# A mixture-of-experts stage on two weight buffers: slots 2 and 3 go to the first buffer, slots 20 and 21 to the second

## The chip, the cores and the metric

The kernel runs on one core of a Trainium2 chip. The metric is the device time of one execution in microseconds. The times before are three runs: 948.5, 950.81 and 951.74 us, median 950.81. The profile is of one further execution that took 946.81 us, of which 945.0 us are the profiled span.

## The reference

Three layers, one after the other: attention, a dense feed-forward layer, and a mixture of experts (the one that the change touches).

```python
scores = scale * np.matmul(q, k.transpose(0, 1, 3, 2))           # 4 x 8 heads, 576 x 64
thresh = np.max(scores, axis=-1, keepdims=True) - tau            # keep what is near the maximum
scores = np.where(scores >= thresh, scores, -1000000000.0)
x = softmax(scores) @ v                                          # -> 2304 tokens x 512
h = x @ w_in;  x = (np.maximum(h, 0.0) + np.log1p(np.exp(-np.abs(h)))) @ w_out   # 512 -> 2048 -> 512
e_idx = np.argmax(x @ w_gate, axis=1)                            # one of 8 experts for each token
for e in range(E):
    mask = e_idx == e
    h = np.maximum(x[mask] @ w1[e], 0.0)                         # 512 x 1024
    ye = h @ w2[e]                                               # 1024 x 512
    out[mask] = gate_w[mask, None] * eom[mask, e, None] * ye
```

## The kernel before

Attention and the feed-forward layer take the first three quarters of the span and are the same in both kernels. The mixture of experts follows. Its tokens are sorted on the chip by expert into slots of up to 128 tokens, each slot with one expert. With these inputs 22 slots run (0 to 21, `MAIN`); three more stand behind a condition (L1374) and are skipped. Slots 0 and 1 (`NPRE`) belong to the expert with the most tokens, chosen before the last two token tiles are routed. The other slots are columns of a table that the kernel computes at about 700 us; column `c` of the table has an expert (`z.esi`), a flag that a new expert begins there (`z.chi`, also set at column `LANE` = 10), and the token numbers (`z.idx`).

One slot goes through these steps:

- `gather` (L1144): GpSimd fetches the slot's rows from DRAM by an indirect transfer into one of five buffers `xg`; `rows` (L1154) transposes them into `xgT` by a transfer on the sync engine's queue.
- `load_w` (L1163): eight transfers of 512 KB on the sync engine's queue, four for the first weight matrix and four for the second, into a ring of 12 raw buffers. They are conditional: where the flag is not set, the transfer is issued without moving anything. A load waits until the conversion that used its raw buffer 12 loads earlier is done.
- `conv_w` (L1178): the conversion of float32 weights into two float16 parts. ScalarE writes the high part (L1195), VectorE the low part (L1200). Both stand in a conditional on the slot's flag (`changed`, L1135), so that they run only where a new expert begins; passing an untaken one costs a branch and an event.
- `up` (L1210): 96 matmuls of 128 columns (L1224) give `hps`; they read all four chunks of the first matrix.
- `relu` (L1234): in two halves, ScalarE (L1238) and then VectorE (L1241) make `hT` in two parts.
- `down` (L1249): 24 matmuls of 512 columns (L1260) give `yps`; block j of eight needs chunk j // 2 of the second matrix.
- `out_y` (L1268): ScalarE scales `yps` into `y` (L1274), GpSimd scatters it to the output (L1277).

There are two buffers of expert weights, `WA` (0) and `WB` (1), each with both matrices. `buf_of` says which slot uses which, `col_of` which column it works on: slots with buffer 0 walk through columns 0 to 9, those with buffer 1 through columns 10 to 19, so that two runs of columns alternate. `before(u)` is the last slot ahead of u with the same buffer; slot u's weights may be written only when that slot's `up` (first matrix) or `down` (second) is done:

```python
u = before(s)
free = (ff1_s, ff2_s)[buf_of(s)][len(groups) - 1] if u is None else (up_s if m == 1 else down_s)[u]
```

A planner (class `Planner`) orders the instructions of each engine from costs and due times, but from slot 2 on (`on`, `FREE`) the order on each engine is that of the code: `chain` makes a step wait for the one called before it on its engine. The loop at L1346 therefore writes the order. In period s stand: the output of slot s-1, the first half of the conversions of slot s+2's first matrix, `up` and the first relu half of slot s+1, the second half of those conversions, the second relu half, the conversions of slot s+1's second matrix, `down` of slot s. TensorE's order is so up(s+1), down(s), up(s+2), down(s+1). `queue` holds the loads in the same order.

Of the kernel before, what the change touches and what calls it, by code (L numbers as in the profile page):

```python
# [49 lines left out]
class Planner:  # L50
# [26 lines left out]
    def at(self, t, fn):  # L77
        self.n += 1
        heapq.heappush(self.events, (t, self.n, fn))
# [77 lines left out]
def attention_ff_moe_kernel(ctx, tc, q, k, v, tau, w_in, w_out, wg, wog, w1, w2, out):  # L157
# [15 lines left out]
    KC = DM // P  # L173
    FC = FF // P
    F2C = F2 // P
    NPRE = 2
# [115 lines left out]
    def step(*a, **kw):  # L292
        return plan[0].step(*a, **kw)
# [673 lines left out]
    MAIN = NU - 3  # L967

    LANE = (MAIN - NPRE) // 2
# [23 lines left out]
    def vec(dur, due, fn, after=(), take=(), drop=()):  # L993
        return step("DVE", dur, due, fn, after, take, drop)
# [109 lines left out]
    flag = {}  # L1104
    queue = []

    def col_of(u):
        return u - NPRE if u >= MAIN else (u - NPRE) // 2 + (LANE if u % 2 else 0)

    def buf_of(u):  # L1110
        return 0 if u <= NPRE else 1 if u >= MAIN else u % 2

    def before(u):

        return next((v for v in range(u - 1, -1, -1) if buf_of(v) == buf_of(u)), None)

    def row_of(u):
        return z.idxp[:, u:u + 1] if u < NPRE else z.idx[:, col_of(u):col_of(u) + 1]

    def when(s):  # L1120
        return D0 + DS * s
# [7 lines left out]
    def chain(on, eng, dur, due, fn, after=(), take=(), drop=(), **kw):  # L1129
        s = step(eng, dur, due, fn, list(after) + ([tail.get(eng)] if on else []), take, drop, **kw)  # L1130
        if on:
            tail[eng] = s
        return s
# [10 lines left out]
    def gather(s, on, after):  # L1144
        xg_b[s] = S_xg.buf(2)

        def fn():
            n = NB * P if s < NPRE else NT
            nc.gpsimd.indirect_dma_start(out=z.xg[s % NG], out_offset=None, in_=x2d[0:n, :], in_offset=bass.IndirectOffsetOnAxis(ap=row_of(s), axis=0),
                                         bounds_check=n - 1, oob_is_err=False)  # L1150

        g_s[s] = chain(on, "POOL", 1.1, when(s) - GAD, fn, after, [xg_b[s]], dma=0.73)

    def rows(s, on):  # L1154
        def fn():
            xgT[s] = z.p2.tile([P, 2 * KC, P], F16, tag="xgT", name="xgT", bufs=XGB)
            nc.sync.dma_start_transpose(out=xgT[s], in_=z.xg[s % NG][:, 0:DM].bitcast(F16))

        b = S_xgT.buf(1)
        n = 2 * KC  # L1160
        tr_s[s] = chain(on, "SP", 0.39 + 0.112 * n, when(s) - XGD, fn, [g_s[s]], [b], [xg_b[s]], dma=0.112 * n), b
# [16 lines left out]
    def conv_w(i, n, on):  # L1178

        ks = range(i, i + n)  # L1180
        m, s, c0 = queue[i]

        def part(k):
            c = queue[k][2]
            w = weights(m, s)
            w = w[:, :, c] if m == 1 else w[:, :, c * JW:(c + 1) * JW]
            r = z.raw[k % RWB]
            return w, r if m == 1 else r.rearrange("p (j d) -> p j d", d=DM)

        sc = SE1 if m == 1 else SE2  # L1190

        def hi():
            for k in ks:
                w, r = part(k)
                nc.scalar.activation(w[:, 0], r, AF.Copy, scale=sc)  # L1195

        def lo():
            for k in ks:
                w, r = part(k)
                nc.vector.scalar_tensor_tensor(out=w[:, 1], in0=r, scalar=sc, in1=w[:, 0], op0=ALU.mult, op1=ALU.subtract)  # L1200

        u = before(s)
        free = (ff1_s, ff2_s)[buf_of(s)][len(groups) - 1] if u is None else (up_s if m == 1 else down_s)[u]
        sd = when(s) - (SPD if m == 1 else SPE) + 0.02 * c0
        a = chain(on, "ACT", n * CVA, sd, lambda: changed("ACT", s, hi), [load_s[k] for k in ks] + [free, flags.get((s, "ACT"))])
        v = chain(on, "DVE", n * CVD, sd, lambda: changed("DVE", s, lo), [a, flags.get((s, "DVE"))])
        for k in ks:
            conv_s[queue[k]] = a, v

    def up(s, on):  # L1210
        xt, t_b = tr_s[s]
        w = [conv_s[1, s, c][1] for c in range(KC) if (1, s, c) in conv_s]
        d = when(s)
        p = up_s.get(s - 1)

        def mm1(hf, i):
            if i == 0:
                hps[s, hf] = z.ps_h.tile([P, 4, P], F32, tag="h", name="hps")
            w1b = weights(1, s)
            for f4 in (2 * i, 2 * i + 1):  # L1220
                c = (4 * hf + f4) * P
                for n in range(3 * KC):
                    wl, xl = THREE[n % 3]
                    nc.tensor.matmul(hps[s, hf][:, f4, :], w1b[:, wl, n // 3, c:c + P], xgT[s][:, xl * KC + n // 3, :], start=n == 0, stop=n == 3 * KC - 1)  # L1224

        for hf in range(2):
            ps_of[s, hf] = S_h.buf(1)
            for i in range(2):
                p = chain(on, "PE", 1.34, d, lambda hf=hf, i=i: mm1(hf, i), [p, xt] + w, [ps_of[s, hf]] if i == 0 else [], [t_b] if hf and i else [])
            h_s[s, hf] = p  # L1230
        up_s[s] = p


    def relu(s, hf, on):  # L1234
        def hi():
            if hf == 0:
                hT[s] = z.p2.tile([P, 2, F2C, P], F16, tag="hT", name="hT")
            nc.scalar.activation(hT[s][:, 0, 4 * hf:4 * hf + 4], hps[s, hf], AF.Relu)  # L1238

        def lo():  # L1240
            nc.vector.scalar_tensor_tensor(out=hT[s][:, 1, 4 * hf:4 * hf + 4], in0=hps[s, hf], scalar=0.0, in1=hT[s][:, 0, 4 * hf:4 * hf + 4],  # L1241
                                           op0=ALU.max, op1=ALU.subtract)

        if hf == 0:
            hT_b[s] = S_hT.buf(1)
        a = chain(on, "ACT", 0.55, when(s), hi, [h_s[s, hf]], [hT_b[s]] if hf == 0 else [])
        hl_s[s, hf] = chain(on, "DVE", 0.6, when(s), lo, [a], drop=[ps_of[s, hf]])
# [20 lines left out]
    def out_y(s, on):  # L1268
        y_b = S_y.buf(1)
        x = {}  # L1270

        def fn():
            x["o"] = z.p2.tile([P, DM], F32, tag="y", name="y")
            nc.scalar.activation(x["o"], hps[s, 2], AF.Copy, scale=z.xg[s % NG][:, DM:DM + 1].bitcast(F32))  # L1274

        def scatter():
            nc.gpsimd.indirect_dma_start(out=out, out_offset=bass.IndirectOffsetOnAxis(ap=row_of(s), axis=0), in_=x["o"], in_offset=None,  # L1277
                                         bounds_check=NT - 1, oob_is_err=False)

        a = chain(on, "ACT", 0.57, when(s) + DND, fn, [down_s[s]], [y_b], [y_ps[s], xg_b[s]])  # L1280
        y_s[s] = chain(on, "POOL", 1.1, when(s) + DND, scatter, [a], drop=[y_b], dma=0.73)
# [7 lines left out]
    def slot_flag(s, name, eng):  # L1289
        c = col_of(s)  # L1290
        flag[name, s] = eng.value_load(z.chi[0:1, c:c + 1], min_val=0, max_val=1)
# [15 lines left out]
    s = step("PE", 0.39, -1, pre_rows, [ps] + oh_s[:NB], [f_b])  # L1307
    s = vec(0.47, -1, pre_index, [s], drop=[f_b])
# [4 lines left out]
    s = vec(1.2, -1, table_slots, [te])  # L1313
    s = vec(0.55, -1, table_ones, [s])
    f_b = S_f.buf(1)
    s = step("PE", 0.5, -1, table_rows, [s] + oh_s, [f_b])
    ti = vec(0.64, -1, table_index, [s], drop=[f_b])
    se = vec(2.45, -0.5, slot_experts, [ti])
    table = [ti, opened] + [x2_w[t] for t in range(NTT)]
# [9 lines left out]
    def fill():  # L1329

        while len(load_s) < min(len(conv_s) + RWB, len(queue)):
            i = len(load_s)
            expert_of(queue[i][1])
            load_w(i, True)

    def convs(m, s, c, on):
        if (m, s, c) in queue:
            conv_w(queue.index((m, s, c)), 2, on)
            fill()


    for s in range(1, MAIN):
        queue += [(1, s + 2, c) for c in range(KC) if s + 2 < MAIN] + [(2, s + 1, c) for c in range(KC) if NPRE < s + 1 < MAIN]
    for i in range(0, 2 * KC, 2):
        conv_w(i, 2, False)
    for s in range(NPRE - 4, MAIN):  # L1346
        on = s >= FREE
        if s > 0:
            out_y(s - 1, on)
        if s + 4 < MAIN:  # L1350
            gather(s + 4, True, table)
        if NPRE <= s + 3 < MAIN:
            rows(s + 3, True)
        if s >= 0:
            fill()
        if s >= 1:
            convs(1, s + 2, 0, on)
        if 0 <= s + 1 < MAIN:
            up(s + 1, on)
            relu(s + 1, 0, on)  # L1360
        if s >= 1:
            convs(1, s + 2, 2, on)
        if 0 <= s + 1 < MAIN:
            relu(s + 1, 1, on)
        if s >= 1:
            for c in range(0, KC, 2):
                convs(2, s + 1, c, on)
        if s >= 0:
            down(s, on)
    out_y(MAIN - 1, True)  # L1370
# [54 lines left out]
```

## Time and profile before

| what | value |
|---|---|
| median of three runs | 950.81 us (948.5 to 951.74) |
| profiled execution | 946.81 us, span 945.0 us |
| TensorE (PE) busy | 803.4 us, 85% of the span |
| VectorE (DVE) busy | 640.5 us, 68% |
| ScalarE (ACT) busy | 601.0 us, 64% |
| GpSimd (POOL) busy | 477.1 us, 50% |

Busy shares are means over stages with different limits, so the change is looked for in its own stage, from about 700 us on. In the page's second part each digit is the busy share of 1/40 of the span (23.6 us) in tenths; `PEclk` is the clock granted to TensorE in tenths of full speed. In a timeline the number in brackets is the idle time of the engine ahead of the row and what ended it.

### The profile page before, as it was taken

What the parts mean: (1) busy time and instruction counts of PE and PEld (TensorE: products, weight loads), DVE (VectorE), ACT (ScalarE), POOL (GpSimd) and SP (SyncE); (2) the same over time, 40 slices, a digit from 0 to 9 for tenths busy, and PEclk for the clock granted to TensorE, in tenths of its full rate; (3) what the DMA queues carried; (4) which work ended last, traced back from release to release, by engine and by line L of the source; (5) the groups of instructions that cost most, each with busy time, mean ns of one, the idle gap of its engine ahead of it and who ended that gap; (6) DMA issues with size and microseconds to landing.
All of it is one profiled execution on the core that took longest, in us unless ns stands there. A gap on an engine that the chain in (4) does not pass through costs nothing. (4 is left out here: it accounts for less than half of the span.)

```text
span 945.0 us, 24188 instructions
## 1 busy us (share of the span) xinstructions
PE 803.4 (85%) x9138; PEld 562.4 (60%) x9138; DVE 640.5 (68%) x1403; ACT 601.0 (64%) x1000; POOL 477.1 (50%) x522
## 2 busy tenths in 40 slices
PE   1244677899889998999999999999894999999996
PEld 0023545567666665666666666666564777777774
DVE  3999999868898788777668575643672335239632
ACT  3665678777787877887777778745522335248532
POOL 2698787667676665775656757532211111122101
PEclk9997779999999999999999999999996999999998
DMA  9989877899999789877876675711729378399970
GB/s 206 238 195 213 207 178 166 170 151 176 199 174 182 139 161 178 166 136 119 146 133 109 126 151 82 127 38 34 235 61 272 106 259 182 93 266 350 253 213 34
DMA packets 353391, 156.45 MB, mean 166 GB/s; under 512 B 314350, under 2 KB 330734, under 8 KB 353264
## 3 DMA queue, kind: packets, MB, share of 16 engines
q1 hardware_dynamic: 349744, 145.33, 72.3%
q0 software_dynamic: 3520, 9.48, 3.6%
q8 instruction: 73, 1.20, 0.5%
q14 instruction: 54, 0.44, 0.2%
HBM read 120.66 MB, written 10.52 MB: 139 GB/s over the span
## 5 line engine op out<-in xcount | busy, mean ns | idle before, releaser
L695 PE MATMUL ph<-xT,WA 128*128 128x128 f16 (+1 forms) x2304 | 212.9, 252 | 14.6 <-ACT r L718 14.1
L591 POOL TENSOR_TENSOR es<-e,es 128x576 f16<-128x576 f32 x144 | 191.7, 1337 | 66.1 <-ACT es L587 61.9
L695 PEld LDWEIGHTS <-WA 128*128 128x128 f16 x2304 | 186.4, 101 | 44.9 <-issue 18.2
L705 PE MATMUL x2ps<-WB,gt 128*128 128x512 f16 x840 | 201.3, 382 | 1.9 <-POOL gt L733 1.1
L558 PE MATMUL sc<-kT,qT 128*128 128x512 f16 (+1 forms) x312 | 90.3, 401 | 71.3 <-DVE e L580 46.6
L580 DVE SCALAR_TENSOR_TENSOR e<-sc,th,e 128x576 f32<-128x576 f32 x140 | 112.0, 813 | 35.0 <-ACT e L575 25.6
L565 DVE TENSOR_REDUCE mx<-sc 128x1 f32<-128x576 f32 x140 | 102.2, 750 | 40.6 <-PE sc L559 37.6
L705 PEld LDWEIGHTS <-gt 128*128 128x128 f16 x840 | 75.5, 98 | 84.2 <-issue 3.9
L733 POOL TENSOR_TENSOR gt<-r,gt 128x512 f16<-128x512 f32 x70 | 83.7, 1196 | 79.5 <-ACT gt L730 71.1
L587 ACT ACTIVATE es<-e 128x576 f16<-128x576 f32 x144 | 98.0, 681 | 31.4 <-DVE e L580 24.3
L575 ACT ACTIVATE e<-sc,nb 128x576 f32<-128x576 f32 x140 | 99.8, 735 | 25.2 <-DVE nb L568 19.2
L1277 POOL DMA_INDIRECT out_dram<-y,idx x20 | 21.6, 1079 | 181.5 <-ACTq L1141 100.5
L603 PE MATMUL pv<-V,eT 128*128 128x64 f16 (+1 forms) x2400 | 85.3, 198 | 21.8 <-DMA eT<-es 16.4
L603 PEld LDWEIGHTS <-eT 128*128 128x128 f16 (+1 forms) x2400 | 80.2, 103 | 35.1 <-DMA eT<-es 26.0
L1241 DVE SCALAR_TENSOR_TENSOR hT<-hps,hT 128x512 f16<-128x512 f32 x44 | 30.2, 689 | 98.4 <-ACTq L1141 66.7
L558 PEld LDWEIGHTS <-qT 128*128 128x128 f16 (+1 forms) x320 | 30.1, 103 | 111.5 <-DVE e L580 45.7
L571 POOL TENSOR_SCALAR th<-mx,tau_s 128x1 f32<-128x1 f32 x144 | 65.2, 457 | 47.1 <-DVE mx L565 38.0
L1260 PEld LDWEIGHTS <-hT 128*128 128x128 f16 x528 | 50.6, 98 | 56.9
L1224 PE MATMUL hps<-xgT,WA 128*128 128x128 f16 x1152 | 69.0, 223 | 10.0 <-DMA xgT<-xg 9.9
L1224 PEld LDWEIGHTS <-WA 128*128 128x128 f16 x1152 | 67.6, 100 | 13.4 <-DMA xgT<-xg 9.5
L727 DVE SCALAR_TENSOR_TENSOR r<-l,r 128x512 f32<-128x512 f32 x72 | 58.1, 807 | 20.7 <-ACT l L724 20.5
L1238 ACT ACTIVATE hT<-hps 128x512 f16<-128x512 f32 x44 | 26.2, 596 | 70.3 <-PE hps L1224 69.9
(171 smaller groups left out, 1318.1 us busy)
## 6 DMA issues: line engine op xcount, KB each, us to landing
raw<-in_moe_w_dram SPq DMA_DIRECT2D x160, 512.0 KB
raw<-in_moe_w_in_dram SPq DMA_DIRECT2D x16, 512.0 KB
raw<-in_moe_w_out_dram SPq DMA_DIRECT2D x16, 512.0 KB
x2d<-row SPq DMA_DIRECT2D x18, 258.0 KB
rawq<-in_q_dram SPq DMA_DIRECT2D x16, 256.0 KB
rawk<-in_k_dram SPq DMA_DIRECT2D x12, 256.0 KB
rawv<-in_v_dram SPq DMA_DIRECT2D x24, 128.0 KB
eT<-es SPq DMA_TRANSPOSE x72
```

The lines of the kernel that those rows point to most:

```text
L558: nc.tensor.matmul(sc[r:r + n, o], w, main[:, :, :, h // 2, o].rearrange("p m x s -> p (m x) s"), start=pa == 0, stop=pa == 1)
L565: nc.vector.tensor_reduce(out=x["mx"], in_=x["sc"], axis=AX.X, op=ALU.max)
L571: nc.gpsimd.tensor_scalar(out=x["th"], in0=x["mx"], scalar1=tau_s, scalar2=None, op0=ALU.subtract)
L575: nc.scalar.activation(x["e"], x["sc"], AF.Exp, bias=x["nb"], scale=SCORE)
L580: nc.vector.scalar_tensor_tensor(out=x["e"], in0=x["sc"], scalar=x["th"], in1=x["e"], op0=ALU.is_ge, op1=ALU.mult, accum_out=sums[t][:, h: ...
L587: nc.scalar.activation(w["e"][:, 0, o * S:(o + 1) * S], x["ev"], AF.Copy)
L591: nc.gpsimd.tensor_tensor(out=w["e"][:, 1, cols], in0=x["ev"], in1=w["e"][:, 0, cols], op=ALU.subtract)
L603: nc.tensor.matmul(pv[t][r:r + n, h, :], eT[u][:, el, j + 4 * o, r:r + n], V[b][:, h // 2, j + 5 * o, vl, :], start=i == 0, stop=i == len( ...
L695: nc.tensor.matmul(ph[:, ci * w * P:(ci + 1) * w * P], WA[:, wl, k // 3, fc * P:(fc + 1) * P], xT[u[0]][:, xl * KC + k // 3], start=k == 0 ...
L705: nc.tensor.matmul(acc_ps[u[a]], gt[:, gl, c:c + P], WB[:, wl, fc, :], start=fc == 0 and m == 0, stop=fc == FC - 1 and m == 2)
L733: nc.gpsimd.tensor_tensor(out=gt[:, 1], in0=r, in1=gt[:, 0], op=ALU.subtract)
L1224: nc.tensor.matmul(hps[s, hf][:, f4, :], w1b[:, wl, n // 3, c:c + P], xgT[s][:, xl * KC + n // 3, :], start=n == 0, stop=n == 3 * KC - 1)
```

## The change

It assigns buffers and columns anew. Slots up to 2 have buffer 0, as before. Before, slot 3 had buffer 1, slot 4 buffer 0, and so on to slot 21 with buffer 1. Now slot 3 has buffer 0 as well, slot 4 buffer 1, slot 5 buffer 0, in turn to slot 19 with buffer 0 and slot 20 with buffer 1, and slot 21 has buffer 1 too. Columns follow: buffer 0 serves columns 0 to 9 with slots 2, 3, 5, 7, ..., 19 (before: 2, 4, ..., 20), buffer 1 columns 10 to 19 with slots 4, 6, ..., 20, 21 (before: 3, 5, ..., 21). Where a slot follows directly on another of its buffer (3 and 21), `in_period` puts its conversions one period later, since its buffer is in use until then. Gathers and scatters at the start come in another order.

```diff
+    def buf_of(u):
+        return 0 if u <= NPRE else 1 if u >= MAIN - 1 else (u - NPRE + 1) % 2
+
     def col_of(u):
-        return u - NPRE if u >= MAIN else (u - NPRE) // 2 + (LANE if u % 2 else 0)
-
-    def buf_of(u):
-        return 0 if u <= NPRE else 1 if u >= MAIN else u % 2
+        if u >= MAIN:
+            return u - NPRE
+        return sum(buf_of(v) == buf_of(u) for v in range(NPRE, u)) + (LANE if buf_of(u) else 0)
...
-    for s in range(1, MAIN):
-        queue += [(1, s + 2, c) for c in range(KC) if s + 2 < MAIN] + [(2, s + 1, c) for c in range(KC) if NPRE < s + 1 < MAIN]
+    def in_period(m, s):
+
+        def at(u):
+            near = before(u) == u - 1
+            return u - 2 + near if m == 1 else u - 1 + near
+
+        return [u for u in range(NPRE + 1, MAIN) if at(u) == s]
+
+    for s in range(MAIN):
+        queue += [(m, u, c) for m in (1, 2) for u in in_period(m, s) for c in range(KC)]
...
-        if s + 4 < MAIN:
-            gather(s + 4, True, table)
+        for u in {-1: (2,), 0: (3,), 1: (4,), 2: (5, 6)}.get(s, (s + 4,) if s > 2 else ()):
+            if u < MAIN:
+                gather(u, True, table)
...
-        if s >= 1:
-            convs(1, s + 2, 0, on)
+        w1s = [(u, c) for u in in_period(1, s) for c in range(0, KC, 2)]
+        n = sum(u == s + 1 for u, c in w1s) or 1
+        for u, c in w1s[:n]:
+            convs(1, u, c, on)
         if 0 <= s + 1 < MAIN:
             up(s + 1, on)
             relu(s + 1, 0, on)
-        if s >= 1:
-            convs(1, s + 2, 2, on)
+        for u, c in w1s[n:max(n, 2)]:
+            convs(1, u, c, on)
         if 0 <= s + 1 < MAIN:
             relu(s + 1, 1, on)
-        if s >= 1:
+        for u, c in w1s[2:]:
+            convs(1, u, c, on)
+        for u in in_period(2, s):
             for c in range(0, KC, 2):
-                convs(2, s + 1, c, on)
+                convs(2, u, c, on)
```

On ScalarE at the start of the stage, before: behind both relu halves of slot 2 (`hT`) stand slot 3's conversions into `WB`, then those of slot 4 into `WA`, ahead of the first relu half of slot 3. Each pair of conversions is in a conditional.

```order
L1238 ACTIVATE hT<-hps 128x512 x2
L1141 COMPARE_AND_BRANCH
L1195 ACTIVATE WB<-raw_10220 128x1024
L1195 ACTIVATE WB<-raw_10221 128x1024
L1141 UNCONDITIONAL_BRANCH x2
...
L1195 ACTIVATE WA<-raw_10212 128x1024
L1195 ACTIVATE WA<-raw_10213 128x1024
L1141 UNCONDITIONAL_BRANCH x5
L1238 ACTIVATE hT<-hps 128x512
```

The same place now: slot 3's conversions go into `WA`, and slot 4's, into `WB`, come behind both relu halves of slot 3 (the second `hT` row), followed by the output of slot 2.

```order
L1240 ACTIVATE hT<-hps 128x512 x2
L1143 COMPARE_AND_BRANCH
L1197 ACTIVATE WA<-raw_10220 128x1024
L1197 ACTIVATE WA<-raw_10221 128x1024
L1143 UNCONDITIONAL_BRANCH x2
...
L1240 ACTIVATE hT<-hps 128x512 x2
L1143 COMPARE_AND_BRANCH
L1197 ACTIVATE WB<-raw_10212 128x1024
L1197 ACTIVATE WB<-raw_10213 128x1024
...
L1276 ACTIVATE y<-yps,xg_10227 128x512
```

What moved: the conversion into `WB` stands one relu further back, and that into `WA` is for a slot that follows slot 2 in the same buffer.

On ScalarE at the end, before: `xg_10228` marks the output of slot 18, `xg_10229` that of 19, `xg_10225` of 20 and `xg_10226` of 21. Slot 21's first matrix (raw 10216 to 10219) is converted around slot 20's relu, its second (raw 10212 to 10215) ahead of the output of slot 20.

```order
L1274 ACTIVATE y<-yps,xg_10228 128x512
L1141 COMPARE_AND_BRANCH
L1195 ACTIVATE WB<-raw_10216 128x1024
...
L1238 ACTIVATE hT<-hps 128x512
...
L1274 ACTIVATE y<-yps,xg_10229 128x512
L1238 ACTIVATE hT<-hps 128x512 x2
L1141 COMPARE_AND_BRANCH
L1195 ACTIVATE WB<-raw_10212 128x1024
...
L1274 ACTIVATE y<-yps,xg_10225 128x512
L1274 ACTIVATE y<-yps,xg_10226 128x512
```

The same place now, from the output of slot 19 on.

```order
L1276 ACTIVATE y<-yps,xg_10229 128x512
L1143 COMPARE_AND_BRANCH
L1197 ACTIVATE WB<-raw_10220 128x1024
...
L1197 ACTIVATE WB<-raw_10223 128x1024
L1143 UNCONDITIONAL_BRANCH x3
L1240 ACTIVATE hT<-hps 128x512 x2
L1276 ACTIVATE y<-yps,xg_10225 128x512
L1143 COMPARE_AND_BRANCH
L1197 ACTIVATE WB<-raw_10212 128x1024
...
L1276 ACTIVATE y<-yps,xg_10226 128x512
```

What moved: slot 21's first matrix (raw 10220 to 10223) is now converted behind the output of slot 19, and its second (raw 10212 to 10215) behind the output of slot 20.

## Rows read from the trace of the kernel before

**Rows 1.** The page's second part: busy tenths of TensorE, and its clock, in 40 slices
```profile
PE   1244677899889998999999999999894999999996
...
PEclk9997779999999999999999999999996999999998
```

**Rows 2.** Busy time by stretch: stretch, length, engines, granted clock, DMA share, GB/s
```profile
715.00:720.00 5.00, 4.22 (x40) 4.22 (x41) 0.00 (x0) 0.00 (x0) 0.00 (x0) 0.50 1.06 239
...
740.00:915.00 175.00, 175.00 (x2008) 128.52 (x2007) 82.64 (x86) 81.62 (x103) 36.38 (x32) 1.00 0.82 229
```

**Rows 3.** Timeline of TensorE at the end: start us, length us, engine, line, operation, tiles
```profile
910.70 5.52 PE L1224 MATMUL hps<-xgT,WA 128*128 128x128 f16 x96
916.06 5.34 PE L1260 MATMUL yps<-WB,hT 128*128 128x512 f16 x24
921.24 5.52 PE L1224 MATMUL hps<-xgT,WB 128*128 128x128 f16 x96
...
931.78 5.34 PE L1260 MATMUL yps<-WB,hT 128*128 128x512 f16 x24
```

**Rows 4.** Timeline of TensorE at the start of the stage
```profile
715.78 7.87 PE L1224 MATMUL hps<-xgT,WA 128*128 128x128 f16 x96 [9.04 <-DMA xgT<-xg]
725.29 0.29 PE L1224 MATMUL hps<-xgT,WB 128*128 128x128 f16 x2 [1.63 <-ACT WB L1195]
...
730.11 6.93 PE L1224 MATMUL hps<-xgT,WB 128*128 128x128 f16 x85 [0.63 <-DVEq L1141]
736.88 5.34 PE L1260 MATMUL yps<-WA,hT 128*128 128x512 f16 x24
742.06 5.52 PE L1224 MATMUL hps<-xgT,WA 128*128 128x128 f16 x96
```

**Rows 5.** Timeline of VectorE at the start of the stage
```profile
724.23 1.29 DVE L1241 SCALAR_TENSOR_TENSOR hT<-hps,hT 128x512 f16<-128x512 f32 x2 [14.52 <-issue]
725.43 4.62 DVE L1200 SCALAR_TENSOR_TENSOR WB<-raw,WB 128x1024 f16<-128x1024 f32 x4
734.98 0.69 DVE L1241 SCALAR_TENSOR_TENSOR hT<-hps,hT 128x512 f16<-128x512 f32 x1 [4.92 <-ACTq L1141]
737.71 0.69 DVE L1241 SCALAR_TENSOR_TENSOR hT<-hps,hT 128x512 f16<-128x512 f32 x1 [2.04 <-ACT hT L1238]
738.66 4.63 DVE L1200 SCALAR_TENSOR_TENSOR WB<-raw,WB 128x1024 f16<-128x1024 f32 x4 [0.25 <-ACT WB L1195]
...
748.25 0.69 DVE L1241 SCALAR_TENSOR_TENSOR hT<-hps,hT 128x512 f16<-128x512 f32 x1 [1.99 <-ACTq L1141]
```

**Rows 6.** Timeline of ScalarE at the end
```profile
910.96 0.69 ACT L1274 ACTIVATE y<-yps,xg 128x512 f32<-128x512 f32 x1 [4.64 <-PE yps L1260]
911.54 1.99 ACT L1195 ACTIVATE WB<-raw 128x1024 f16<-128x1024 f32 x2
...
921.50 0.69 ACT L1274 ACTIVATE y<-yps,xg 128x512 f32<-128x512 f32 x1 [4.64 <-PE yps L1260]
...
927.30 3.89 ACT L1195 ACTIVATE WB<-raw 128x1024 f16<-128x1024 f32 x4
```

**Rows 7.** Line 1141 from 745 to 750 us: count, ns min/median/max, first and last start
```profile
L1141 DVEq EVENT_SEMAPHORE  x4: 21/21/21, 746.3 to 749.6; - x4
```

**Rows 8.** Timeline of ScalarE at the start of the stage
```profile
724.18 3.88 ACT L1195 ACTIVATE WB<-raw 128x1024 f16<-128x1024 f32 x4
...
737.58 3.88 ACT L1195 ACTIVATE WB<-raw 128x1024 f16<-128x1024 f32 x4
```

**Rows 9.** Timeline of the sync engine's queue, slots 3 and 4
```profile
715.70 4.97 SPq L1171 DMA_DIRECT2D raw<-in_moe_w_dram  x8
```

**Rows 10.** Timeline of TensorE, 680 to 688 us
```profile
681.35 0.60 PE L705 MATMUL x2ps<-WB,gt 128*128 128x512 f16 x2 [0.72 <-ACT gt L730]
683.11 4.02 PE L705 MATMUL x2ps<-WB,gt 128*128 128x512 f16 x10 [1.15 <-POOL gt L733]
```

**Rows 11.** Line 1200 from 905 to 945 us
```profile
L1200 DVE SCALAR_TENSOR_TENSOR WB<-raw,WB x8: 1215/1218/1226, 912.6 to 931.8; 128x1024 f16<-128x1024 f32 x8
```

## The prediction

> **What bounds the kernel now.** I read the page's forty slices first, because the change touches only the last quarter of the span. TensorE's row is full nearly everywhere; one slice, the 31st (709 to 732 us), shows 4 tenths, and TensorE's clock row shows 6 there [rows 1]. Next came the table by stretches: from 740 to 915 us TensorE is busy 175.00 of 175.00 us at a granted clock of 1.00 [rows 2]. So once the slots run, TensorE alone sets the time, at 10.54 us a slot: 5.36 us for a first product (910.70 to 916.06) and 5.18 us for a second (916.06 to 921.24) [rows 3]. I call them up(n) and down(n) for slot n. Everything else is hidden there, and this change can be worth something only at the two ends of the stretch.
>
> The timeline of TensorE shows the front end [rows 4]. up(2) waits 9.04 us for its gathered, transposed rows and then takes 7.87 us, against 5.52 us for the same 96 matmuls later on: it runs largely at the lower of the clock's two levels, 1.2 of 2.4 GHz (granted clock 0.50 from 715 to 720 us [rows 2]). up(3) is the first product on the second buffer pair. It waits in pieces for ScalarE's and VectorE's conversion of that expert's weights, and 85 of its 96 matmuls start only at 730.11, when VectorE's last conversion (725.43 + 4.62) is done [rows 5]. down(2) starts at 736.88, up(4) at 742.06, and 5.36 us later, at 747.42, up(4) is through. At the back end TensorE has no idle time before its last matmul at 931.78 + 5.34 = 937.1 [rows 3], although slot 21 changes expert: ScalarE's timeline shows its first-product weights converted from 911.54 and its second-product weights from 927.30, both beside TensorE's work [rows 6].
>
> **The start.** The change gives slot 3 to the first buffer pair, whose expert is already there. That no new expert comes at the place it takes (column 1) shows in the trace: between 734.98 and 737.71 VectorE has no conversion for the old slot 4 [rows 5]. So up(3) no longer waits for loaded weights. It waits for VectorE to pass two conditionals that are not taken, and these stand behind the second half of slot 2's relu, which ends at 724.23 + 1.29 = 725.52 [rows 5]. Passing is cheap: after a relu that ended at 748.25 + 0.69 = 748.94 the last event of the conditionals is at 749.6, 0.66 us for what is at least two of them [rows 5, 7]. Bounds 0 and 0.7; I take 0.4, and up(3) starts at 725.9. At full clock it ends 5.36 us later, at 731.3.
>
> Next late is the conversion itself, now for slot 4 and, by the order, behind both halves of slot 3's relu on ScalarE. The same sequence stands in the trace for another matrix: TensorE ends up(3) at 736.88, ScalarE starts converting at 737.58, VectorE ends the last at 738.66 + 4.63 = 743.29, which is 6.41 us after the product [rows 4, 5, 8]. So slot 4's first-product weights are ready at 737.7. down(2) covers 5.18 us of the 6.41. With 85 matmuls still to do (85/96 of 5.36 = 4.75) up(4) ends at 742.4, against 747.42 now: 5.0 us gained.
>
> Are the weights there by then? The sync engine's row puts eight loads, slot 3's four and slot 4's four, into 715.70 to 720.67 [rows 9]; the first one issued is read by ScalarE at 724.18 [rows 8], so landing takes at most 8.5 us. Slot 4's, the last of them issued by about 720.7, are there by 729.2, before ScalarE comes to them (731.3 + 0.7 = 732.0). Slot 4's other matrix must now wait for raw buffers that this conversion frees; issued by 737.7 and landed by 746.2, it is converted in 5.7 us (738.66 + 4.63 - 737.58) by 751.9, and down(4) is due at 742.4 + 5.18 + 5.36 = 753.0. down(3) and up(5) hide it with 1.1 us to spare; what is later than that is lost in full. Of the moved gathers and scatters one pair changes places on GpSimd, the second scatter and slot 5's gather; slot 5 is not needed before 747, so I cost this at nothing (bounds from both sides half of one microsecond, in what the other transfers do to slot 2's rows).
>
> What could lower the gain is the clock. up(3) now starts after a gap of 2.2 us. The nearest row is at 681 to 683 us, where two gaps of 0.72 and 1.15 us came before ten matmuls that took 4.02 us [rows 10]; at full clock ten take about 2.3 (24 take 5.34). There the clock fell and cost 1.7 us. Here the idle time is about as much, but TensorE was busy without a break before it. The rows do not decide this, so I take the middle of 3.3 and 5.0: **4.1 us gained**. An upper bound is 7.2 (up(3) right behind up(2), at 723.65).
>
> **The end.** Slots 20 and 21 now stand in the same buffer pair. Slot 21's new weights may overwrite slot 20's only after up(20) and after down(20), and by ScalarE's order both conversions stand behind an output that waits for a second product: the first-product weights behind the output of slot 19, so behind down(19); the second-product weights behind the output of slot 20, so behind down(20). Nothing is left to cover them, since TensorE's order is up(20), down(19), up(21), down(20), down(21). I count from the end of a second product: the output starts 0.26 us later (921.24 to 921.50), the first conversion follows the output's start by 0.58 (910.96 to 911.54) [rows 3, 6], and VectorE's fourth ends 5.71 us after that (737.58 to 743.29) [rows 5, 8].
> - Gap before up(21): 0.26 + 0.58 + 5.71 = 6.55 us, less 0.61 for the eleven matmuls that, as in up(3) now, slip in between: 5.94.
> - up(21) then runs on a fallen clock. up(2) paid 7.87 - 5.52 = 2.35 us for 96 matmuls [rows 4]; 85 of 96 make 2.1. Bounds 1.7 (the ten matmuls above) and 2.5.
> - Gap before down(21): its first two of eight blocks need only one chunk, so 0.26 + 0.58 + (738.66 - 737.58) + 1.22 for one VectorE conversion = 3.14 us [rows 5, 8, 11]. The chunks behind it come faster than TensorE takes them (4.63 us for four against 5.18).
> - down(21) on a fallen clock: nearest is again the 1.7 us after 1.9 us of gaps; bounds 0 and 2.5.
>
> The Trainium skill, in "TensorE: Matmul & The Clock Gate" (section "Wait — 56ns, not 53.3ns?"), gives 426.7 ns between starts of 512-column matmuls at 1.2 GHz and 215.7 at 2.4; by it the whole of down(21) at the lower level would cost 24 x 0.211 = 5.1 us, an estimate that no run here shows.
>
> **The sum.** 5.94 + 2.1 + 3.14 + 1.7 = 12.9 us lost at the end, 4.1 gained at the start, in between TensorE stays full: +8.8 us. The other changes of expert move to slots 4, 8, 10, 13, 15, 16 and 18 from 3, 7, 9 and 14 to 17; four in a row are hidden now [rows 2], so two in a row are. What follows the last matmul (945.0 - 937.1 = 7.9 us) is taken as unchanged. The profiled execution goes from 946.81 to 955.6; it lies 4.0 below the median of the three timed runs (950.81), so the median becomes 950.81 + 8.8 = **959.6 us**.
>
> **Rivals.**
> - The clock costs nothing at any of the three places: 5.94 + 3.14 - 5.0 = +4.1, 954.9 us. Against it: 2.35 us in up(2) [rows 4] and 1.7 us after much shorter gaps [rows 10]. The same page of the Trainium skill (section "What's actually happening") says that for modelling, the penalty of the ramp is under 1% of a typical span and not worth fitting. In size the trace agrees: 2.35 of 945 us is 0.25%. But this change is itself under 1%, and by that rule the sum would be the 954.9 of this rival. Chance 0.15.
> - The gain at the start fails and the end is as forecast: slot 4's weights come late or the clock falls for all of up(3) and up(4). Gain 1 us or less: +11.9 or more, 962.7. For it: the thin cover and the lower clock from 725 on that the 31st slice shows [rows 1]. Chance 0.15.
> - Faster: the last column brings no new expert, so that slot 21's conditionals are not taken. Then both gaps vanish, only 4.1 us gained remain: 946.7. It decides at one flag, that of column 19, which slot 21 reads before and after. Against it: the conversions at 911.54 and 927.30 [rows 6]. Chance 0.03.
> - Even: gain near its upper bound (7.2) with little clock loss at the end: 5.94 + 3.14 + 0.5 - 7.2 = +2.4, 953.2. Chance 0.06.
> - The forecast, with clock terms between their bounds, keeps 0.61; its own range is 956 to 962.
>
> **Numbers.** From the bounds: least 5.94 + 1.7 + 0 + 3.14 - 5.0 = +5.8, most 5.94 + 2.5 + 3.14 + 2.5 - 3.3 = +10.8; with the scatter of the timed runs (948.5 to 951.74) and part of the first two rivals I give 954.5 to 963.5. A measurement of this kernel tells about 0.3%, 2.9 us, from no change. Slower by more: 0.61 + 0.15 + 0.15 and a little of the even case, 0.92; within: 0.05; faster: 0.03.
>
> **What would show it.** In TensorE's timeline of the changed kernel: up(3) beginning near 726 without a wait for loaded weights, up(4) ending near 742 to 744; no idle time from there to up(20); then two gaps, some 6 us before the 85 last matmuls of up(21), put down to VectorE's conversion, and some 3 us before the last second product; ScalarE's conversions right behind the outputs of slots 19 and 20. I am wrong if TensorE has no gap behind up(20), if conversions show behind slot 2, or if idle time turns up between slots 5 and 20.

## The result, and the profile after

The changed kernel takes 958.57 us (median of four runs, 958.51 to 958.92) against 950.09 us (four runs, 948.5 to 951.74): a ratio of 1.0090 [1.0071, 1.0109]. The profiled execution took 958.92 us with a span of 957.1. It lies 0.35 us above its median, while the one of before (946.81) lies 3.3 us under its own, so the two traces differ by 12.1 us and the medians by 8.5. Both kernels were timed once more side by side: 958.23 against 948.56 us, 1.0108 [1.0094, 1.0123]. The forecast of +8.8 us stands among these differences. Of all executions reported below one, in e3, took far longer than the others of its kernel (1099.73 us); it counts in the median given there and not in the ratio.

TensorE's timeline of the changed kernel at the start of the stage, to be laid beside [rows 4]. Lines of the code stand two higher than before. The last matmuls that the change cannot touch, those into `tk`, start at 705.48 here and at 704.82 in the trace of before, so 0.66 us are older than the change.

```profile
705.48 0.60 PE L1072 MATMUL tk<-OHS,OHP 128*128 128x23 f16 x18
...
715.13 8.30 PE L1226 MATMUL hps<-xgT,WA 128*128 128x128 f16 x96 [7.74 <-DMA xgT<-xg]
724.17 0.28 PE L1226 MATMUL hps<-xgT,WA 128*128 128x128 f16 x2 [0.73 <-ACTq L1143]
726.60 7.05 PE L1226 MATMUL hps<-xgT,WA 128*128 128x128 f16 x94 [2.14 <-DVEq L1143]
733.48 5.34 PE L1262 MATMUL yps<-WA,hT 128*128 128x512 f16 x24
738.66 0.78 PE L1226 MATMUL hps<-xgT,WB 128*128 128x128 f16 x11
739.94 4.92 PE L1226 MATMUL hps<-xgT,WB 128*128 128x128 f16 x85 [0.51 <-DVEq L1143]
745.59 0.38 PE L1262 MATMUL yps<-WA,hT 128*128 128x512 f16 x1 [0.73 <-ACTq L1143]
746.33 5.12 PE L1262 MATMUL yps<-WA,hT 128*128 128x512 f16 x23 [0.36 <-DVEq L1143]
```

up(3) now reads `WA`, and the "<-WB" rows of [rows 4] are gone. Its 94 last matmuls begin at 726.60 and wait for VectorE's conditionals only. They take 7.05 us for work that takes 5.4 at full clock. up(4) is now the first product on `WB`. And down(3) waits twice (745.59, 746.33), where down(2) and down(3) of before waited for nothing.

VectorE in the same stretch, same columns, beside [rows 5]:

```profile
725.19 1.29 DVE L1243 SCALAR_TENSOR_TENSOR hT<-hps,hT 128x512 f16<-128x512 f32 x2 [14.82 <-ACTq L1143]
...
735.26 4.63 DVE L1202 SCALAR_TENSOR_TENSOR WB<-raw,WB 128x1024 f16<-128x1024 f32 x4 [0.26 <-ACT WB L1197]
...
745.53 0.69 DVE L1243 SCALAR_TENSOR_TENSOR hT<-hps,hT 128x512 f16<-128x512 f32 x1 [1.30 <-ACTq L1143]
```

The conversion that stood at 725.43 is gone; slot 4's is at 735.26 and ends at 739.89, 0.05 us before up(4) goes on. That is 6.41 us after up(3)'s end at 733.48, the very sequence that the prediction read from another matrix. What held VectorE until 725.19 is told by the line that reads the flags (operation, count, duration in ns least/median/most, first and last start us):

```profile
L1293 DVEq TENSOR_LOAD <-chi x19: 298/308/1219, 710.2 to 724.5; - x19
...
L1293 DVEq SEQ_ASSERT  x19: 23/23/41, 711.1 to 725.1; - x19
```

VectorE reads 19 flags into registers, one after the other, from 710.2 to 725.1, and slot 2's relu stands behind them. Before, the same 19 reads ended at 724.2, and the relu of [rows 5] at 724.23 stood right behind them too.

The end of the stage on TensorE, beside [rows 3]:

```profile
915.49 5.34 PE L1262 MATMUL yps<-WA,hT 128*128 128x512 f16 x24
922.61 0.29 PE L1226 MATMUL hps<-xgT,WB 128*128 128x128 f16 x2 [1.78 <-ACT WB L1197]
923.87 0.34 PE L1226 MATMUL hps<-xgT,WB 128*128 128x128 f16 x3 [0.97 <-DVE WB L1202]
...
927.27 7.44 PE L1226 MATMUL hps<-xgT,WB 128*128 128x128 f16 x85 [0.64 <-DVE WB L1202]
934.55 5.34 PE L1262 MATMUL yps<-WB,hT 128*128 128x512 f16 x24
941.66 0.38 PE L1262 MATMUL yps<-WB,hT 128*128 128x512 f16 x1 [1.77 <-ACT WB L1197]
942.92 6.75 PE L1262 MATMUL yps<-WB,hT 128*128 128x512 f16 x23 [0.88 <-DVE WB L1202]
```

ScalarE there, beside [rows 6]:

```profile
920.92 0.69 ACT L1276 ACTIVATE y<-yps,xg 128x512 f32<-128x512 f32 x1 [4.64 <-PE yps L1262]
921.51 3.88 ACT L1197 ACTIVATE WB<-raw 128x1024 f16<-128x1024 f32 x4
...
939.98 0.69 ACT L1276 ACTIVATE y<-yps,xg 128x512 f32<-128x512 f32 x1 [4.63 <-PE yps L1262]
940.57 3.88 ACT L1197 ACTIVATE WB<-raw 128x1024 f16<-128x1024 f32 x4
```

Both conversions of slot 21 stand right behind the outputs of slots 19 and 20, and TensorE waits for each. In before they ran at 911.54 and 927.30 beside its work.

Last, the table by stretches (stretch, length, busy time of the five engines, granted clock, DMA share, GB/s), beside [rows 2]:

```profile
727.80:731.20 3.40, 3.40 (x36) 3.40 (x34) 0.00 (x0) 0.48 (x1) 0.00 (x0) 0.50 0.55 122
...
745.00:907.00 162.00, 161.00 (x1810) 116.64 (x1810) 81.34 (x83) 77.27 (x98) 32.64 (x29) 1.00 0.82 222
...
925.80:932.60 6.80, 5.83 (x54) 5.57 (x55) 1.95 (x3) 0.60 (x1) 0.00 (x0) 0.50 0.01 2
942.80:946.30 3.50, 3.38 (x9) 1.16 (x9) 3.48 (x4) 1.65 (x2) 0.00 (x0) 0.51 0.08 27
```

Between the ends TensorE stays full: 161.00 of 162.00 us, and the missing microsecond is the wait at down(3). At three places besides up(2) the granted clock is at the lower level: in up(3), in up(21) and in down(21).

So the traces differ by 0.66 us ahead of the change, by a gain of 1.23 us from there to the end of up(20) (210.01 us from `tk` against 211.24), by a loss of 13.1 us from there to TensorE's last matmul (949.67 - 915.49 = 34.18 against 937.12 - 916.06 = 21.06), and by 0.45 us less behind it (7.43 against 7.88): 0.66 - 1.23 + 13.12 - 0.45 = 12.1.

### The profile page after: what moved, and what is told of

It reads as the page before. It is cut to its first block, busy times and chain, and to the rows that moved or that the text cites. A ratio compares the mean times of both kernels' runs of the same rounds, so it can differ in the third digit from the quotient of the medians.

```text
span 957.1 us, 24194 instructions
## 1 busy us (share of the span) xinstructions
PE 807.5 (84%) x9138; PEld 564.9 (59%) x9138; DVE 639.6 (67%) x1403; ACT 599.7 (63%) x1000; POOL 476.4 (50%) x522
## 5 line engine op out<-in xcount | busy, mean ns | idle before, releaser
L695 PE MATMUL ph<-xT,WA 128*128 128x128 f16 (+1 forms) x2304 | 212.7, 252 | 15.4 <-ACT r L718 15.0
L1226 PE MATMUL hps<-xgT,WA 128*128 128x128 f16 x1152 | 71.4, 226 | 12.1 <-DMA xgT<-xg 9.2
L1202 DVE SCALAR_TENSOR_TENSOR WB<-raw,WB 128x1024 f16<-128x1024 f32 x48 | 55.9, 1220 | 25.8 <-ACT WB L1197 25.6
```

The costliest lines, as they stand in the source:

```text
L695: nc.tensor.matmul(ph[:, ci * w * P:(ci + 1) * w * P], WA[:, wl, k // 3, fc * P:(fc + 1) * P], xT[u[0]][:, xl * KC + k // 3], start=k == 0 ...
```

## The experiments

All ratios are to the kernel before on the same chip, with a 95% interval. Runs up to e4 shared one chip, e5 to e8 a second, e9 to e12 a third; diffs are against the changed kernel.

**The start without the end.** Slot 21 goes back to the first buffer, so that the slots of the second pair are 4, 6, ..., 20 and the columns split 11 to 9.

```diff
-    LANE = (MAIN - NPRE) // 2
+    LANE = (MAIN - NPRE) // 2 + 1
-        return 0 if u <= NPRE else 1 if u >= MAIN - 1 else (u - NPRE + 1) % 2
+        return 0 if u <= NPRE else 1 if u >= MAIN else (u - NPRE + 1) % 2
```

> The columns are split 11 to 9, so that slot 21 stands in buffer 0 (column 10, no new expert) and slot 20 alone takes column 19's expert; the start stays as in the changed kernel. Theory (the loss is the two conversions of slot 21 behind slot 20 in one buffer): both gaps at the end vanish, 34.2 us from the end of up(20) become 21; what stays is the start, 1 to 2 us better than before: 947 to 949 us. Rival (the loss comes with the other places of the expert changes, 4, 8, 10, 13, ...): these stay nearly as they are, so 955 or more.

Measured: 945.27 us, 0.9978 [0.9966, 0.9991]. TensorE has no idle time behind down(3) to the end, and the loss of 13 us is gone, so the rival, by which the moved changes of expert cost, falls. What is left is the start alone: 2.1 us by the ratio, about half of the 4.1 forecast.

**The end without the start.** Slots 2 to 18 alternate as before, the gathers too; 19 takes the first buffer, 20 and 21 the second.

```diff
-        return 0 if u <= NPRE else 1 if u >= MAIN - 1 else (u - NPRE + 1) % 2
+        return 0 if u <= NPRE or u == MAIN - 3 else 1 if u >= MAIN - 2 else u % 2
-        for u in {-1: (2,), 0: (3,), 1: (4,), 2: (5, 6)}.get(s, (s + 4,) if s > 2 else ()):
+        for u in (s + 4,):
```

> The end alone: slots 3 to 18 and the gathers as in the kernel before, slots 18 and 19 both in buffer 0 (no new expert at 19), 20 and 21 both in buffer 1. Theory: the loss at the end, 13 us, comes back in full, plus about 1 us for slot 19's conditionals that stand close to their use: 962 to 965 us. Rival (the loss needs the changed start): 950 us.

Measured: 963.33 us, 1.0161 [1.0144, 1.0179], 15.3 us over before by the ratio. TensorE's timeline of this run:

```profile
902.87 5.53 PE L1226 MATMUL hps<-xgT,WA 128*128 128x128 f16 x96 [0.88 <-ACTq L1143]
...
919.67 0.38 PE L1262 MATMUL yps<-WA,hT 128*128 128x512 f16 x1 [0.73 <-ACTq L1143]
920.41 5.12 PE L1262 MATMUL yps<-WA,hT 128*128 128x512 f16 x23 [0.36 <-DVEq L1143]
...
931.98 7.34 PE L1226 MATMUL hps<-xgT,WB 128*128 128x128 f16 x85 [0.63 <-DVE WB L1202]
...
947.53 6.70 PE L1262 MATMUL yps<-WB,hT 128*128 128x512 f16 x23 [0.88 <-DVE WB L1202]
```

The gaps of slot 21 come back in full without the change at the start. The first three rows are a second cost, of which the prediction counted only what stands ahead of up(3), at 0.4 us: two slots in a row in one buffer make TensorE wait even where no conversion runs, 0.88 us at the first product and 1.1 at the second. Their releasers are the conditionals (L1143) that ScalarE and VectorE pass untaken. A product that follows without a wait starts 0.16 us before the end of the one ahead (916.06 against 910.70 + 5.52 in [rows 3]), so each wait costs that much more than its idle time. With it the rows give 2.4 us for slot 19 and 13.0 for slot 21, 15.4 against the 15.3 of the ratio.

**The first gap closed.** Slot 21's first-matrix conversions are put ahead of slot 19's output.

```diff
+        ahead = [(u, c) for u in in_period(1, s) if u == s + 1 == MAIN - 1 for c in range(0, KC, 2)]
+        for u, c in ahead:
+            convs(1, u, c, on)
```

> The changed kernel with the conversions of slot 21's first matrix ahead of slot 19's output on ScalarE and VectorE. Theory (the first gap is mostly the order, since the conversion waits behind an output that waits for down(19)): conversion starts about 1.1 us after up(20) instead of 6, ends 6.9 after it, and down(19) covers 5.2: gap 1.7 instead of 6.6 and no fallen clock in up(21), together 7 us less: 951 to 953 us. Rival (the buffer is in use until then anyway, the order costs nothing): 958 us as it is.

Measured: 951.19 us, 1.0032 [1.0020, 1.0045]. Its timeline:

```profile
922.91 4.92 PE L1226 MATMUL hps<-xgT,WB 128*128 128x128 f16 x85 [0.79 <-DVE WB L1202]
927.66 5.34 PE L1262 MATMUL yps<-WB,hT 128*128 128x512 f16 x24
934.78 0.38 PE L1262 MATMUL yps<-WB,hT 128*128 128x512 f16 x1 [1.77 <-ACT WB L1197]
936.03 6.81 PE L1262 MATMUL yps<-WB,hT 128*128 128x512 f16 x23 [0.88 <-DVE WB L1202]
```

up(21) now runs at full clock almost behind down(19), the second gap and its fallen clock are as they were. That ScalarE's order, behind an output that itself waits for down(19), makes the first gap is shown; by the ratios (1.0032 against 1.0090 and 1.0108) it and its clock are worth 5.5 to 7.2 us of the 13; in the trace the stretch from the end of up(20) to the last matmul takes 27.07 us against 34.18, 7.1 less.

**Slot 21 without a new expert.** The flag of column 19 is cleared, so that slot 21's loads and conversions are left out and it computes with slot 20's expert.

```diff
+        f.memset(z.chi[:, MAIN - NPRE - 1:MAIN - NPRE], 0)
```

> The changed kernel with the flag of column 19 set to zero, so that slot 21 computes with slot 20's expert: its loads and conversions are left out. Theory: the conversions themselves are the gaps; passing the conditionals behind the outputs of 19 and 20 leaves about 1.5 us of each: 13 us of loss become 3: 948 to 950 us. Rival (the order of waits alone makes the gaps, with or without work in them): 955 or more.

Measured: 947.36 us, 0.9997 [0.9985, 1.0009]. The two places in its timeline:

```profile
921.32 5.53 PE L1227 MATMUL hps<-xgT,WB 128*128 128x128 f16 x96 [0.88 <-ACTq L1144]
...
932.90 5.34 PE L1263 MATMUL yps<-WB,hT 128*128 128x512 f16 x24 [0.87 <-ACTq L1144]
```

The loss hangs on the taken flag, as the prediction's third rival had it, but without it the kernel would still not be faster: passing the untaken conditionals behind the two outputs lets TensorE wait 0.88 + 0.87 us, and the stretch from the end of up(20) to the last matmul takes 23.15 us, 2.1 more than before (3 were expected) and about what the start gives.

**The flags out of the way.** On the version of e1, flags of later slots are read five slots ahead and not all before slot 2's relu.

```diff
-... lambda name=name, eng=eng: slot_flag(s, name, eng), [se])
+... lambda name=name, eng=eng: slot_flag(s, name, eng), [se, hl_s.get((s - 5, 1))])
```

> The 11 to 9 split, and the reading of the flags of slots 7 and later on ScalarE and VectorE deferred until the relu of five slots earlier, so that VectorE reads 4 flags ahead of slot 2's relu and not 19. Theory (up(3) waits 2.1 to 3.6 us because VectorE reads 19 flags first, and the clock falls for that gap): the gap shrinks to 1.5 to 2 us, up(3) runs at full clock or nearly: 1.5 to 3.5 us less than with the split alone, 942 to 944 us. Rival (VectorE's relu and passes alone make the gap): as with the split alone, 945 us.

Measured: 941.56 us, 0.9926 [0.9911, 0.9940]. Its up(3):

```profile
726.12 5.42 PE L1226 MATMUL hps<-xgT,WA 128*128 128x128 f16 x94 [0.51 <-DVEq L1143]
```

The gap ahead of up(3) is 0.51 us (3.34 in e1's trace, 2.14 in after's), and the clock stays full: 5.42 us for 94 matmuls (7.94 in e1's). So the register reads set the start of up(3), and the gap that they make brings the clock down. By the two ratios this is worth 0.52%, 4.9 us, more than the 1.5 to 3.5 expected; e1 was timed on another chip.

**The passes out of the way.** On e1, where a slot in a row needs no new weights for its second product, its conditionals are put ahead of the next slot's product.

```diff
+        near2 = [u for u in in_period(2, s) if u == s < MAIN - 1]
+        for u in near2:
+            for c in range(0, KC, 2):
+                convs(2, u, c, on)
```

> The 11 to 9 split, and the untaken conditionals of slot 3's second matrix put ahead of up(4) and slot 4's relu on ScalarE and VectorE. Theory (down(3) waits 1.1 us in two pieces since these conditionals stand behind slot 4's relu): both pieces vanish, 1.4 us less than with the split alone, 944 us. Rival (down(3) waits for the relu or its clock): as with the split alone, 945 us, and the pieces stay.

Measured: 945.65 us (940.51 to 949.51), 0.9972 [0.9956, 0.9988]. In its trace down(3) follows up(4) with no wait, but up(6) now waits:

```profile
747.81 5.34 PE L1262 MATMUL yps<-WA,hT 128*128 128x512 f16 x24
...
764.74 0.29 PE L1226 MATMUL hps<-xgT,WB 128*128 128x128 f16 x2 [0.24 <-ACT WB L1197]
766.00 4.92 PE L1226 MATMUL hps<-xgT,WB 128*128 128x128 f16 x85 [0.97 <-DVE WB L1202]
```

So the place of the passes causes the wait at down(3). Its worth can't be told: e1 had 0.9978 and the intervals overlap. The trace is of the slowest of the twelve executions: its gap ahead of up(3) was longer (4.48 us), and the 1.2 us at up(6), where ScalarE waits for slot 6's loads, appear neither in e1's trace nor in those of e8 and e12, which have the moved passes too. In time this one is inconclusive.

**The clock at the end.** Behind down(19) and behind down(20), TensorE gets matmuls of 512 columns whose result nobody reads, 26 and 11 of them, so that it isn't idle there.

```diff
+            for i in range(n):
+                nc.tensor.matmul(t, xgT[s][:, 4, :], xgT[s][:, 0:4, :], start=i == 0, stop=i == n - 1)
...
+            warm(26, MAIN - 1, True)
...
+            warm(11, MAIN - 1, True)
```

> The changed kernel with matmuls that nobody reads in the two gaps at the end: 26 of 512 columns ahead of up(21), 11 ahead of down(21). Theory (4.0 of the 13.1 us at the end are the clock that falls for the gaps, 2.5 in up(21) and 1.5 in down(21)): both products run at full clock and the gaps keep their length: 4 us less than the changed kernel, 954 to 955 us. Rival (the products are slow for another reason, such as conversions on the other engines beside them): 958 us as it is.

Measured: 956.10 us, 1.0086 [1.0065, 1.0106]. It was not timed beside the changed kernel (1.0090), and the two intervals overlap, so it decides nothing; both were run again together.

> The changed kernel once more, beside the one with matmuls in its gaps, on one chip: 0.9% above the kernel before, 13 us lost from the end of up(20) on and 1 to 3 us gained ahead of it.

> The changed kernel with matmuls that nobody reads in the two gaps at the end, once more, because the first timing was compared with the changed kernel on another chip. Theory (the fallen clock is 4 of the 13 us): 0.4% less than the changed kernel on this chip. Rival (what the clock gives back at the end is lost elsewhere): the same time.

Measured: the changed kernel 958.23 us, 1.0108 [1.0094, 1.0123]; with the unread matmuls 956.01 us, 1.0071 [1.0058, 1.0084]. The intervals don't touch; the difference of the ratios is 0.37%, 3.5 us (that of the medians 2.2). TensorE's timeline of the latter:

```profile
922.13 5.78 PE L1276 MATMUL warm<-xgT 128*128 128x512 f16 x26
...
928.75 4.92 PE L1226 MATMUL hps<-xgT,WB 128*128 128x128 f16 x85 [0.22 <-DVE WB L1202]
933.50 5.34 PE L1262 MATMUL yps<-WB,hT 128*128 128x512 f16 x24
938.68 2.54 PE L1276 MATMUL warm<-xgT 128*128 128x512 f16 x11
...
941.87 5.12 PE L1262 MATMUL yps<-WB,hT 128*128 128x512 f16 x23 [0.44 <-DVE WB L1202]
```

The same places in the changed kernel on that chip (e10):

```profile
926.95 7.06 PE L1226 MATMUL hps<-xgT,WB 128*128 128x128 f16 x85 [0.63 <-DVE WB L1202]
...
942.21 6.54 PE L1262 MATMUL yps<-WB,hT 128*128 128x512 f16 x23 [0.88 <-DVE WB L1202]
```

The weights are no earlier, but the 85 matmuls take 4.92 us, not 7.06, and the 23 take 5.12, not 6.54: 3.6 us of clock in the two traces (4.2 against the first trace of the changed kernel, with 7.44 and 6.75). The prediction's first rival, by which the clock costs nothing, falls.

**All of it at the start.** e1, e5 and e6 together, and 30 unread matmuls behind down(1), ahead of up(2).

```diff
+        if s == 1:
+            warm(30, 1, False, [down_s[1]])
```

> The 11 to 9 split with the deferred flags, the conditionals ahead of up(4), and 30 matmuls of 512 columns that nobody reads in the wait ahead of up(2). Theory (start: up(2) at a fallen clock costs 1.3 to 2.8 us, the gap ahead of up(3) and its clock 3 to 5, down(3)'s waits 1.4): 5 us less than the split alone, 939 to 941 us. Rival (the matmuls delay up(2), or the parts overlap): 943 us or more.

Measured: 937.46 us, 0.9885 [0.9867, 0.9902], the fastest version here. Its start:

```profile
715.32 5.53 PE L1226 MATMUL hps<-xgT,WA 128*128 128x128 f16 x96 [1.06 <-DMA xgT<-xg]
721.71 0.28 PE L1226 MATMUL hps<-xgT,WA 128*128 128x128 f16 x2 [0.85 <-ACTq L1143]
722.50 5.42 PE L1226 MATMUL hps<-xgT,WA 128*128 128x128 f16 x94 [0.51 <-DVEq L1143]
727.76 5.34 PE L1262 MATMUL yps<-WA,hT 128*128 128x512 f16 x24
...
739.21 5.34 PE L1262 MATMUL yps<-WA,hT 128*128 128x512 f16 x24
```

up(2) takes 5.53 us (8.30 in after) and down(3) waits for nothing. The time is below the 939 to 941 us expected. The same without the 30 matmuls:

> The best version without its 30 matmuls ahead of up(2): 11 to 9 split, deferred flags, conditionals ahead of up(4). Theory (the matmuls hold the clock for up(2), which takes 5.5 us with them and 7 to 8 without): 1.5 to 2.5 us above the best version, 0.9905 to 0.9915 of the kernel before. Rival (the deferred flags and conditionals do all of it): 0.9885.

Measured: 941.88 us, 0.9928 [0.9912, 0.9944], so that the unread matmuls are worth 0.43% by the two ratios (on two chips), about 4 us, more than the 1.5 to 2.5 expected. Of that up(2)'s own row explains 2.7 (8.20 against 5.53 us). Against e5's 0.9926 the moved passes again show nothing in time, though the wait is gone from the trace.

**The kernel before once more**, for the scatter:

> The kernel before once more, for a second profile of it: the first one (946.81 us) lies below the median of the timed runs. Theory (executions differ by where the clock falls between up(2) and up(4), and in the attention stage ahead of it): the end from up(20) on takes 21.1 us again, the stretch from the end of down(1) to the start of down(3) differs from 40.7 us by up to 2. Rival (the end varies): the end differs by more than 0.5.

Measured: 948.09 us, 0.9996 [0.9986, 1.0006]. Its trace shows the end exactly as before (21.06 us from the end of up(20) to the last matmul) and a start within 0.4 us of it. So the 13 us at the end aren't scatter. Ahead of the change executions do differ: `tk` starts at 704.63 us in e7's trace and at 705.88 in e11's, which are one kernel, and between 703.76 (e1) and 707.59 (e5) in all traces. The 2 to 3 us by which both traces of before lie under their medians are in executions that no trace shows.

## Why the prediction was right, and where not

**What bounds it**: right. TensorE set the time, full from 747 to 915 us, and the change acted at the two ends alone; the changes of expert one slot earlier or later, the moved gather and scatter, and slot 4's second matrix (converted from 745.98, due only after 756) cost nothing, as said.

**The end, 12.9 us forecast, 13.1 measured** (12.5 in the second pair of traces, 33.59 us in e10 against 21.06 in e9). This is shown: it comes back alone (e2), goes with the buffer (e1) and with the flag (e4). By terms: the gap before up(21) lasted 920.67 to 927.27, 6.60 us against 6.55, less the same eleven matmuls. The clock in up(21) cost 7.44 - 4.92 = 2.5 against 2.1, at its upper bound (2.1 in e10's trace). down(21) ended 9.94 us after down(20) (949.67 - 939.73), 4.60 over its 5.34, against 3.14 + 1.7 = 4.84. The chain of steps read from other matrices of before (output, high part, low part) carried over to within 0.1 us.

**The start, 4.1 us forecast, 1.2 to 2.3 measured: the mis-sized term.** up(3) began when forecast (726.60, against 725.9 plus the 0.66 that lay ahead), and slot 4's weights came 6.41 us after it, as forecast. The relu that sets up(3)'s start was taken over from the trace of before; that 19 flag reads set the relu, the prediction did not see. But the clock fell and cost 1.5 us of up(3) (733.48 - 726.60 = 6.88 against 5.36), near the upper bound, where the middle of 0 and 1.7 was taken. At up(4)'s end the gain from `tk` on was so 3.4 us (742.06 + 5.52 - 704.82 = 42.76 before, 739.94 + 4.92 - 705.48 = 39.38 now), at the lower bound of 3.3. Then 1.4 us went at down(3), with waits of 0.73 and 0.36 us, a step that the prediction lacked: it priced the passing of slot 3's first conditionals and not of its second, which stand behind slot 4's relu, with nothing beside them. A further 0.7 us went between up(5) and up(20), where six first products took 5.55 to 5.73 us and not 5.52, with no idle time listed. The second trace of before has 0.4 us of the same and e1's none, so it isn't shown to come from the change; its cause stays open. e1 puts the whole start at 2.1 us by its ratio, and the second pair of traces at 2.3 (212.00 us from `tk` to the end of up(20) in e9, 209.74 in e10).

**The sum.** +8.8 was forecast, 8.5 and, in the later timing, 9.7 us were measured. From `tk` to the last matmul the two pairs of traces give 11.9 and 10.3 us, so the end was right to 0.2 to 0.4 us and the start 2 to 3 us too good. That the first medians come nearer to the forecast is luck: the traced execution of before lies 3.3 us under its median and that of after does not, and what makes the other executions of before longer is not seen. In the later timing the ratio (1.0108, 10.2 us) and the traces agree. The mechanism was forecast rightly at the end and, but for the wait at down(3), at the start; the total is nearer than the terms deserve.

**Rivals.** "The clock costs nothing" fell (e10 and e11). The Trainium skill's remark in "TensorE: Matmul & The Clock Gate" (section "What's actually happening"), that "the ramp penalty is <1% of a typical kernel span; don't fit to a specific cold count", holds in size here too (0.37%), yet this is a third of what the change costs on that chip (1.08%). "The gain fails" (1 us or less) is not borne out, though near: the start gave 3.4 us at up(4) and 1.2 and 2.3 at up(20). "Faster by an unset flag" fell twice: the flag is set, and without it the time is even (e4). "Even" fell with the end.

## What to carry to other kernels

Where one engine is full, judge a reordering by its two ends: where a double buffer's uses no longer alternate and the second of two in a row needs new contents, the refill chain is exposed, here 13 us at the end, some 4 of them the clock; 7 of the 13 came back when the first refill was only put ahead of an output in the order (e3). The chain's length can be read from another place where it stands in full. Count for every step in such a row also what its engines merely pass (register reads, untaken conditionals), for these become the wait when the data wait is gone. The gain that the change aims at is to be had without its cost: keep the alternation at the end (e1), and take what then stands at the start out of the way (e5, e8). Whether the deferred flags and the unread matmuls would give as much to the kernel before, without any change of buffers, was not run.

## What the runs showed of the hardware

- A register read from SBUF is long in a row: 19 flags held VectorE from 710.2 to 725.1 us, 0.78 us a flag, with a median of 0.31 us for the load and 0.18 for the register operation behind it, and single loads up to 1.2 us. What fills the rest the rows don't tell.
- TensorE's clock fell to the lower level after a gap of 2.14 us that followed 0.73 us (granted 0.50 from 727.8 to 731.2), and stayed full after gaps of 0.85 and 0.51 us (e5). Unread matmuls in the gaps at the end kept it full (granted 1.00 from 910 to 947 in e11), though they wrote nothing that anyone needs.
- Passing untaken conditionals on ScalarE and VectorE, at some 0.04 to 0.06 us a branch, let TensorE wait 0.88 us at one product and 1.1 at another (e2); where they stood elsewhere in the order, the wait was gone (e6).
